# Splitting a 128-point and 16-point transform as 64 points and 32, with the outer steps in half-array TensorE tiles

## The chip, the cores and the metric

The kernel runs on one core of a Trainium2 chip. The metric is device time in microseconds (us) of one execution; lower is better. Three runs of the kernel before were timed, and one more execution was recorded by the hardware profiler. All times of instructions below are from that one profiled execution.

## The reference

The kernel computes a layer and all its gradients. `x` is `A_q` (2048 rows of 512), `xn` its layer norm. Part A is a long convolution: `kv = shift(k) * v`, where `shift` is a four-tap causal filter over the rows with weights `A_shift_k`; then every one of the 512 columns of `kv` is convolved causally with its own kernel of 2048 taps, the rows of `A_ssm_k`, by Fourier transforms of length 4096. Part B is a gated feed-forward of width 1376.

```
k_shift = sum over t of k_pad[:, t:t+S, :] * shift_k[:, 3-t]
kv      = k_shift * v
y       = irfft(rfft(kv padded to 2S) * rfft(ssm_k padded to 2S))[:S] + kv * ssm_D
out     = x + xn * y + ((xn @ w_gate) * (xn @ w_up)) @ w_down
```

The outputs are `out` and the gradients of `sum(out * grad_out)` by `A_q`, `A_k`, `A_v`, `A_shift_k`, `A_ssm_k`, `A_ssm_D`, `B_w_gate`, `B_w_up` and `B_w_down`. The gradients of the convolution need three transforms forward (the taps, `kv`, and `dy = grad_out * xn`) and three back (for `y`, for the gradient of `kv`, for the gradient of the taps).

## The kernel before

**Layout.** A matrix of 2048 rows lies in SBUF as 128 partitions of 16 rows: row `s = 16 p + r` is row `r` of partition `p` (`nat`, L219). A load of two of the 16 rows for all partitions (`x_n[:, 2b:2b+2, :]`) is one DMA of 128 pieces of 2 KB. Such loads and stores are issued one by one by SP: `x_b`, `go_b` (L302, L307), `v_b` (L353), `xb` (L543), `vb` (L918), and the stores of `kb`, `dk`, `o` and `e` (L947, L1088, L1107, L1122). The tile `kh` (and `khC` later) holds 16 rows of `k` and the 3 rows before them, which are fetched from the neighbour partition by two further DMAs (`load_k`, L310; `load_kh`, L1126); `dks` gets the 3 rows behind its own from the next partition in the same way (L950).

**The transforms.** The transform of 2048 padded rows is split in two steps, 128 points over the partitions `p` and 16 over `r`.

- Stage 1 forward, `stage1` (L361): for each signal and each `r`, two matmuls with the table `W1`, one for the real and one for the imaginary part (`c`). Each contracts 128 partitions, gives 128 frequencies and 512 columns, into one PSUM bank of `pf`. ACT (for some of the taps' rows DVE) copies `pf` to `fst`, and after every second `r` a DMA stores it to the DRAM tile `FD`. There are 3 signals of 16 rows, 96 matmuls (and two more, of one row, that add `ssm_D` for signal 0, L372).
- Stage 2, `groups` (L737): in 8 groups `g` of 16 frequencies. `g_fwd` (L577) loads `X` from `FD` and multiplies by the table `EF` in tiles of 64 rows and 32 columns, eight of them next to each other. A tile holds two frequencies of 32 inputs, and half of `EF` is zero, written by the masks in `forward` (L137). ACT copies `ps` to `SP`, DVE multiplies the spectra (`g_mul`, L592), and `g_inv` (L606) goes back with the table `EI` in tiles of 32 rows and 64 columns, whose other half is zeroed by `inverse` (L181). The result goes to the DRAM tile `GD`.
- Stage 1 back. `st1p` (L909) makes two rows of `y` or of the gradient of `kv`: for each row two matmuls of the table `IW` with `g`, accumulated over real and imaginary part, 512 columns, into `pq`; 64 matmuls in all. `inv_dk` (L961) makes the gradient of the taps, transposed: there `g` is the stationary operand and `IW` the moving one, 128 columns, two accumulated matmuls for each piece of `po`; 128 matmuls.
- `kernel_spec` (L408) transposes the taps into that layout first, 64 transposes `ptk` of 128 by 128, in four groups of 16.

**Tables.** The class `Tables` makes `W1`, `IW`, `EF` and `EI` on the chip: phases as integers by DVE (for the inverse by POOL: `inverse_base`, `inverse_phases`), folded to the period by DVE (`fold`, L72), then a sine on ACT (`sin`, L75), then the masks on DVE.

**Order.** The program is written as generators. `main` (L853) walks the eight row chunks of the feed-forward (`ffn1`, `yb`), and after each piece a `side` generator is advanced: first `front` (L712: norm, filter, stage 1 forward), then `groups`. The last part is `dw` (L1014: the weight gradients, `pu` and `pd`), with four side generators that start and step at fixed counts (L1158): `inv_y`, `dsk_gram`, `inv_dk` and `ew`, the elementwise tail `final` and `bwd` on DVE. The first microseconds run under a manual schedule (L657); elsewhere the framework orders each engine's instructions at build time by program order, readiness and priority (`high_priority`). Every engine and SP's DMA queue then work in that fixed order. PSUM is shared by three two-bank buffers (`P2`) and two one-bank buffers (`P1`); `pf`, `ptk`, `ps`, `pg`, `pq`, `po`, `pu`, `pk` and the transposes `pt` all rotate through `P2`.

Of the kernel before, what the change touches and what calls it, by code (L numbers as in the profile page):

```python
# [10 lines left out]
I32 = mybir.dt.int32  # L11
# [22 lines left out]
class Tables:  # L34


    def __init__(self, nc, tab, spectral, tmp):
# [9 lines left out]
        self.odd = tmp.tile([P, P], F32, name="odd")  # L47
        nc.gpsimd.iota(self.odd[:], [[2, P]], base=1, channel_multiplier=0, **f)
        self.lin = tmp.tile([P, P], F32, name="lin")
        nc.gpsimd.iota(self.lin[:], [[1, P]], base=0, channel_multiplier=0, **f)  # L50
        self.patF = tmp.tile([P, 32, 16], F32, name="patF")
        nc.gpsimd.iota(self.patF[:], [[8, 32], [512, 16]], base=0, channel_multiplier=0, **f)
        self.patR = tmp.tile([P, 16, 16], F32, name="patR")
        nc.gpsimd.iota(self.patR[:], [[0, 16], [1, 16]], base=0, channel_multiplier=0, **f)
        self.patG = tmp.tile([P, 16], F32, name="patG")
        nc.gpsimd.iota(self.patG[:], [[32, 8], [4, 2]], base=0, channel_multiplier=0, **f)
# [20 lines left out]

    def small_phases_w(self):
        nc = self.nc
        tmp = self.tmp  # L80
        self.tiw = tmp.tile([P, 2, P], I32, name="tiw")
        for c, off in enumerate((128, 256)):
            nc.vector.tensor_scalar(self.tiw[:, c, :], self.odd[:], self.pf[:, 0:1], float(off + 256), op0=ALU.mult, op1=ALU.add)
        self.fold(self.tiw, 512)

    def small_phases_v(self):
        nc = self.nc
        tmp = self.tmp
        kk = self.col("kk")
        nc.vector.tensor_scalar(kk[:], self.pf[:], 2.0, 1.0, op0=ALU.mult, op1=ALU.add)  # L90
        self.tiv = tmp.tile([P, 2, P], I32, name="tiv")
        for c, off in enumerate((128, 256)):
            nc.vector.tensor_scalar(self.tiv[:, c, :], self.lin[:], kk[:, 0:1], float(off + 256), op0=ALU.mult, op1=ALU.add)
        self.fold(self.tiv, 512)

    def small_sin_w(self):
        self.W1 = self.tab.tile([P, 2, P], BF, name="W1")
        self.sin(self.W1[:], self.tiw, 512)

    def small_sin_v(self):  # L100
        self.IW = self.tab.tile([P, 2, P], BF, name="IW")
        self.iwf = self.tmp.tile([P, 2, P], F32, name="iwf")
        self.sin(self.iwf[:], self.tiv, 512)

    def small_scale(self):
        self.nc.vector.tensor_scalar(self.IW[:], self.iwf[:], 1.0 / 2048, None, op0=ALU.mult)

    def forward_base(self):
# [3 lines left out]
        self.fr = r = self.icol("fr", 0, 15)  # L112
        c = self.icol("fc", 4, 1)
        k4 = self.icol("fk", 5, 3)
        self.fk2 = self.icol("fk2", 5, 1)
        b = self.col("fb")
        nc.vector.tensor_scalar(b[:], k4[:], 2.0, 1.0, op0=ALU.mult, op1=ALU.add)
# [7 lines left out]
    def forward_phases(self):  # L125
        nc = self.nc
        tmp = self.tmp
        self.tif = tmp.tile([P, 32, 2, 16], I32, name="ti", tag="ti")
        for ri in range(2):
            nc.vector.tensor_scalar(self.tif[:, :, ri, :], self.patF[:], self.fr[:, 0:1], self.base[:, ri:ri + 1], op0=ALU.mult, op1=ALU.add)  # L130
        self.fold(self.tif, 8192)

    def forward_sin(self):
        self.zf = self.tmp.tile([P, 32, 2, 16], BF, name="zf")
        self.sin(self.zf[:], self.tif, 8192)

    def forward(self):  # L137
        nc = self.nc
        self.EF = self.spectral.tile([P, 32, 2, 2, 16], BF, name="EF")
        for q in range(2):  # L140
            mk = self.col(f"fm{q}")
            nc.vector.tensor_scalar(mk[:], self.fk2[:], float(q), None, op0=ALU.is_equal)
            nc.vector.tensor_scalar(self.EF[:, :, :, q, :], self.zf[:], mk[:, 0:1], None, op0=ALU.mult)

    def inverse_base(self):

        e = self.nc.gpsimd
        j = self.icol("gj", 0, 15)
        q4 = self.icol("gq", 5, 3)
        self.gk2 = k2 = self.icol("gk", 4, 1)  # L150
        self.gb = b = self.col("gb")
        e.tensor_scalar(b[:], q4[:], 8.0, 1.0, op0=ALU.mult, op1=ALU.add)
        e.tensor_tensor(b[:], b[:], k2[:], op=ALU.add)
        e.tensor_tensor(b[:], b[:], k2[:], op=ALU.add)
        t = self.col("gt")
        e.tensor_scalar(t[:], j[:], 512.0, None, op0=ALU.mult)
        e.tensor_tensor(b[:], b[:], t[:], op=ALU.add)

    def inverse_phases(self):
# [3 lines left out]
        pa = tmp.tile([P, 16, 16], F32, name="pa")  # L163
        e.tensor_tensor(pa[:], self.patR[:], self.patG[:].unsqueeze(2).to_broadcast((P, 16, 16)), op=ALU.mult)
        pb = tmp.tile([P, 16, 16], F32, name="pb")
        e.tensor_scalar(pb[:], self.patR[:], self.gb[:, 0:1], None, op0=ALU.mult)
        e.tensor_tensor(pb[:], pb[:], pa[:], op=ALU.add)
        self.tii = ti = tmp.tile([P, 16, 2, 2, 16], I32, name="tii")
# [8 lines left out]
    def inverse_sin(self):  # L177
        self.zi = self.tmp.tile([P, 16, 2, 2, 16], BF, name="zi")
        self.sin(self.zi[:], self.tii, 8192)

    def inverse(self):  # L181
        nc = self.nc
        self.EI = self.spectral.tile([P, 16, 2, 2, 32], BF, name="EI")
        for q in range(2):
            mk = self.col(f"gm{q}")
            nc.vector.tensor_scalar(mk[:], self.gk2[:], float(q), None, op0=ALU.is_equal)
# [1010 lines left out]
```

## Time and profile before

| What | us |
|---|---|
| the three timed runs | 487.03, 491.52, 493.36 (median 491.52) |
| span of the profiled execution, first to last instruction | 486.7 (its own time is not given beside the span) |
| PE, DVE, ACT, POOL busy | 473.5, 339.5, 318.0, 14.0 |
| L369 `pf`, stage 1 forward: 96 matmuls of 512 columns, PE busy | 25.7 |
| L913 `pq`, stage 1 back: 64 of 512 | 15.1 |
| L971 `po`, stage 1 back for the taps: 128 of 128 | 8.5 |
| L414 `ptk`, transposes of the taps: 64 | 4.7 |
| L584 `ps` and L613 `pg`, stage 2: 384 each of 512, in tiles | 15.0, 15.7 |
| L143 and L187, masks of `EF` and `EI` on DVE | 1.0 each |

The span counts from the first to the last instruction. A matmul's own duration is longer than the distance to the next, because matmuls are pipelined; so what one costs is read from starts. In a list of groups the columns are: line, engine and operation, output and input by the program's names, partitions by elements and type, count; then busy time, mean ns of one, and the idle time of the engine just before them with what ended it. In a timeline the columns are start, length, engine, line, operation, and in brackets an idle time and what ended it. The chain of work that ended last is followed back from the last instruction, at each step to what released it.

### The profile page before, as it was taken

Reading aid. Unit: us, or ns where it says so; the run is one execution under the profiler, and the core shown is the slowest. Engines: PE = TensorE matmul, PEld = TensorE weight load, DVE = VectorE, ACT = ScalarE, POOL = GpSimd, SP = SyncE. Lnnn points to the kernel's source line nnn. Section 1 sums busy time; section 2 is a strip of 40 time slices with the busy share of each in tenths; the row PEclk is TensorE's granted clock in tenths of the full one; section 3 lists DMA queues with packets and bytes.
Section 4 is the critical chain, followed back from the end, with each engine's and each line's share of the span. In section 5 each row is a group of like instructions: output and inputs, shape, how many; then the busy total and the mean of one; then the engine's idle time right before and its main releaser. Section 6 shows DMA issues by size and latency. Waiting matters only on the chain.

```text
span 486.7 us, 10581 instructions
## 1 busy us (share of the span) xinstructions
PE 473.5 (97%) x4375; PEld 316.7 (65%) x4375; DVE 339.5 (70%) x623; ACT 318.0 (65%) x354; POOL 14.0 (3%) x30
## 2 busy tenths in 40 slices
PE   8999998899999999999999999999999999999997
PEld 7867753546747638547547743566767787788885
DVE  6699969987366566777857876113256999999860
ACT  4688885758757769779879976275676544344331
POOL 4400000000000000000000000001000000000000
PEclk9999999999999999999999999999999999999999
DMA  9999999998996968968978469999999999599746
GB/s 273 374 375 336 304 239 308 327 337 323 314 303 218 244 193 275 278 196 261 300 227 270 141 216 351 358 324 318 324 378 377 345 366 410 199 285 252 231 152 193
DMA packets 105325, 139.87 MB, mean 287 GB/s; under 512 B 33307, under 2 KB 78784, under 8 KB 103742
## 3 DMA queue, kind: packets, MB, share of 16 engines
q1 hardware_dynamic: 103694, 137.84, 86.3%
q10 hardware_dynamic: 1584, 1.36, 1.0%
q8 instruction: 34, 0.56, 0.5%
q14 instruction: 13, 0.11, 0.1%
HBM read 68.45 MB, written 63.41 MB: 271 GB/s over the span
## 4 chain that ended last, share of the span: by engine, by line
PE 63%; DVE 21%; DMA 10%; issue 2%; ACT 1%; POOL 1%; SPq 1%; ACTq 0%; DVEq 0%
PE pgu L511 12%; PE px L555 12%; PE pu L1032 10%; PE py L548 6%; PE pdh L517 6%; PE pd L996 5%; DMA x_b<-in_A_q_dram 3%; PE ps L584 3%; PE pg L613 3%; PE pt L840 2%; DMA out_dram<-o 2%; DMA hb<-HDD 2%; DVE t_b L392 2%; DVE ks_b L393 1%; DVE fst L238 1%
## 5 line engine op out<-in xcount | busy, mean ns | idle before, releaser
L555 PE MATMUL px<-WT,hd 128*128 128x512 bf16 (+1 forms) x352 | 81.0, 380 | 0.0
L1032 PEld LDWEIGHTS <-xnC 128*128 128x128 bf16 x704 | 67.1, 98 | 8.8 <-issue 0.9
L555 PEld LDWEIGHTS <-hd 128*128 128x128 bf16 (+1 forms) x352 | 32.9, 98 | 44.2 <-issue 7.3
L1032 PE MATMUL pu<-natd,xnC 128*128 128x256 bf16 x512 | 58.5, 273 | 0.2 <-ACT nath L235 0.2
L235 ACT CAST GO<-pg 128x1024 bf16<-128x1024 f32 x48 | 46.2, 1015 | 13.4 <-issue 6.7
L511 PE MATMUL pgu<-xt,Wu 128*128 128x256 bf16 (+1 forms) x352 | 53.1, 273 | 1.5 <-ACT gu L235 1.0
L600 DVE TENSOR_TENSOR T<-SP 128x2048 bf16<-128x2048 bf16 x24 | 29.4, 1223 | 34.8 <-ACT SP L235 34.8
L235 ACT CAST SP<-ps 128x1024 bf16<-128x1024 f32 x48 | 46.5, 1026 | 10.3 <-PE ps L584 8.4
L235 ACT CAST gu<-pgu 128x1024 bf16<-128x1024 f32 (+1 forms) x48 | 45.3, 944 | 11.6 <-PE pgu L511 11.3
L511 PE MATMUL pgu<-xt,Wg 128*128 128x256 bf16 (+1 forms) x352 | 52.8, 273 | 0.0
L517 PE MATMUL pdh<-gt,WdT 128*128 128x256 bf16 (+1 forms) x352 | 47.4, 273 | 0.1
L511 PEld LDWEIGHTS <-Wu 128*128 128x128 bf16 (+1 forms) x352 | 33.1, 100 | 16.2 <-issue 11.7
L548 PE MATMUL py<-Wd,hd 128*128 128x512 bf16 (+1 forms) x176 | 41.2, 380 | 0.0
L235 ACT CAST fst<-pf 128x1024 bf16<-128x1024 f32 x40 | 38.9, 1028 | 1.5 <-issue 1.3
L235 ACT COPY natd<-pt 128x2048 bf16<-128x2048 bf16 x16 | 30.0, 1874 | 14.1 <-PE pt L840 14.1
L235 ACT CAST og<-pu 128x1024 bf16<-128x1024 f32 (+1 forms) x11 | 10.9, 993 | 42.2 <-PE pu L1032 37.7
L517 PEld LDWEIGHTS <-WdT 128*128 128x128 bf16 (+1 forms) x352 | 34.8, 100 | 5.3 <-ACT WdT L235 0.2
L511 PEld LDWEIGHTS <-Wg 128*128 128x128 bf16 (+1 forms) x352 | 34.9, 100 | 3.6
L532 DVE TENSOR_TENSOR hd<-gu 128x512 bf16<-128x512 bf16 (+1 forms) x48 | 19.0, 396 | 21.8 <-ACT gu L235 21.6
L533 DVE TENSOR_TENSOR hd<-gu,dh 128x1024 bf16<-128x1024 bf16 (+1 forms) x48 | 30.8, 642 | 1.0
L996 PE MATMUL pd<-goC,nath 128*128 128x512 bf16 x128 | 30.1, 379 | 0.0
L548 PEld LDWEIGHTS <-hd 128*128 128x128 bf16 (+1 forms) x176 | 16.5, 98 | 20.8 <-issue 3.1
(173 smaller groups left out, 700.8 us busy)
## 6 DMA issues: line engine op xcount, KB each, us to landing
HDD<-hd SPq DMA_DIRECT2D x35, 384.0 KB, 4.0
FD<-fst SPq DMA_DIRECT2D x24, 512.0 KB, 4.8
X<-FD SPq DMA_DIRECT2D x24, 512.0 KB, 4.3
GD<-GO SPq DMA_DIRECT2D x24, 512.0 KB, 3.6
g<-GD SPq DMA_DIRECT2D x12, 1024.0 KB, 8.6
hb<-HDD SPq DMA_DIRECT2D x8, 1344.0 KB, 8.1
bb<-BX SPq DMA_DIRECT2D x8, 512.0 KB, 6.3
BX<-bx SPq DMA_DIRECT2D x7, 512.0 KB, 4.0
```

Source lines behind the costliest of these rows:

```text
L235: nc.scalar.copy(o, i)
L511: nc.tensor.matmul(pgu[:w, i, t, :], lhsT=W[:, c, f0:f0 + w], rhs=xt[:, :, c, :], start=(c == 0), stop=(c == NC4 - 1))
L517: nc.tensor.matmul(pdh[:w, i, :], lhsT=WdT[:, c, f0:f0 + w], rhs=gt[:, :, c, :], start=(c == 0), stop=(c == NC4 - 1))
L532: nc.vector.tensor_tensor(hd[:fw, fb0:fb0 + n, 0, :], gu[:fw, :n, 0, :], gu[:fw, :n, 1, :], op=ALU.mult)
L533: nc.vector.tensor_tensor(hd[:fw, fb0:fb0 + n, 1:3, :], gu[:fw, :n], dh[:fw, :n].unsqueeze(2).to_broadcast((fw, n, 2, 256)), op=ALU.mult)
L548: nc.tensor.matmul(py[:], lhsT=hd[:fw, fb, 0, ss], rhs=Wd[:fw, fb, :], start=(fb == 0), stop=(fb == NFB - 1))
L555: nc.tensor.matmul(px[:], lhsT=hd[:fw, fb, t, ss], rhs=W[:fw, fb, :], start=(t == 1 and fb == 0), stop=(t == 2 and fb == NFB - 1))
L584: nc.tensor.matmul(ps[32 * q:32 * q + 32, a, :], lhsT=TB.EF[64 * a:64 * a + 64, 4 * g + q, ri].rearrange("p k j -> p (k j)"), rhs=X[64 * a ...
L600: tt(W[:].rearrange("p c a d -> p c (a d)"), A[:, i:i + 1].rearrange("p c a d -> p c (a d)").to_broadcast((P, 2, 2 * D)), B[:].rearrange(" ...
L613: nc.tensor.matmul(pg[q // 2][64 * a:64 * a + 64, q % 2, :], lhsT=TB.EI[32 * q:32 * q + 32, 2 * g + a, yi].rearrange("p k c -> p (k c)"), ...
L996: nc.tensor.matmul(pd[:fw, :], lhsT=nat_h(fb, r), rhs=goC[:, r, :], start=(r == 0), stop=(r == R - 1))
L1032: nc.tensor.matmul(pu[:, c, :, :fw], lhsT=xnC[:, r, cs(c)], rhs=nat_d(fb, r), start=(r == 0), stop=(r == R - 1))
```

## The change

The split becomes 64 points, then 32: row `s = 32 p + 16 h + r` with 64 values of `p`, two of `h` and 16 of `r`, and `h` and `p` together lie on the 128 partitions (`h` selects the half). What follows from it:

- Every load and store of rows becomes two DMAs of 64 partitions (`load_rows`, `store_rows`); the pieces stay 2 KB. The halo of `kh` and `dks` takes three DMAs instead of two. A transposed load of `grad_out` from DRAM becomes two of 64 rows; that of `xn` stays one.
- Stage 1 forward: for each row, two matmuls that contract 64 partitions each, for `h = 0` and `h = 1`, into two banks; one matmul gives the real and imaginary part of 64 frequencies. The count of matmuls and their 512 columns stay.
- Stage 1 back: in `st1p` two matmuls contract 128 partitions each and give 64 outputs, for `h = 0` in the lower and `h = 1` in the upper half of PSUM, with nothing accumulated. In `inv_dk` each matmul has 64 moving columns instead of 128, and writes every second number of `po`.
- The transposes of the taps become 128 of 64 outputs, in the two halves of PSUM.
- `EF` and `EI` are dense: the sine writes them directly, with twice the numbers, and the masks go. Tile shapes and counts of stage 2 stay.
- `inverse_base` and `inverse_phases` are called ahead of the first statistics instead of behind `forward_phases`.

```diff
-        return ap.rearrange("(p r) d -> p r d", r=R)
+        return ap.rearrange("(p h r) d -> h p r d", h=2, r=R)
+    def load_rows(t, src, rb):
+        for h in range(2):
+            nc.sync.dma_start(t[hs(h)], src[h, :, rb, :])
+    def store_rows(dst, rb, t):
+        for h in range(2):
+            last = nc.sync.dma_start(dst[h, :, rb, :], t[hs(h)])
...
-        for c in range(2):
-            point = sig == 0 and r == 0
-            nc.tensor.matmul(pf[:, c, :], lhsT=TB.W1[:, c, :], rhs=src[:, i, :], start=True, stop=not point)
+        for h in range(2):
+            point = sig == 0 and r == 0 and h == 0
+            nc.tensor.matmul(pf[:, h, :], lhsT=TB.W1[hs(h)].rearrange("p k c -> p (k c)"), rhs=src[hs(h), i, :], start=True, stop=not point)
...
-                    src = ssk[:, c, :].rearrange("d (p r) -> d r p", r=R)[:, r0 + i, :]
-                    nc.tensor.transpose(pt[:, i, cs(c)], src, ident[:])
+                    for h in range(2):
+                        src = ssk[:, c, :].rearrange("d (p h r) -> d h r p", h=2, r=R)[:, h, r0 + i, :]
+                        nc.tensor.transpose(pt[hs(h), i, cs(c)], src, ident[:])
...
-            xs, gs = XN[:, rb, :], go_n[:, rb, :]
-        for t, src in ((xt, xs), (gt, gs)):
-            nc.sync.dma_start_transpose(out=t[:].rearrange("p r c s -> p (r c) s"), in_=src.rearrange("p r d -> p (r d)"))
+            xs, gs = XN[:, rb, :], (go_n[0, :, rb, :], go_n[1, :, rb, :])
+        for t, src, ss in ((xt, xs, slice(0, P)), *((gt, g, slice(P // len(gs) * h, P // len(gs) * (h + 1))) for h, g in enumerate(gs))):
+            nc.sync.dma_start_transpose(out=t[:].rearrange("p r c s -> p (r c) s")[:, :, ss], in_=src.rearrange("p r d -> p (r d)"))
...
     TB.forward_base()
+    TB.small_base()
+    TB.inverse_base()
+    TB.inverse_phases()
     norm_stats(0)
...
     TB.forward_phases()
-    TB.inverse_base()
-    TB.inverse_phases()
...
-            TB.forward()
...
-            TB.inverse()
...
-            for c in range(2):
-                nc.tensor.matmul(pq[:, i, :], lhsT=TB.IW[:, c, :], rhs=g[:, c, i0 + i, :], start=(c == 0), stop=(c == 1))
+            for h in range(2):
+                nc.tensor.matmul(pq[hs(h), i, :], lhsT=TB.IW[:], rhs=g[:, h, i0 + i, :], start=True, stop=True)
...
-                DKS[r0] = nc.sync.dma_start(o3_n[:, r0:r0 + 2, :], kb[:])
+                DKS[r0] = store_rows(o3_n, slice(r0, r0 + 2), kb)
...
-                po = P2("po", [P, 2, 4, P])
-                for h in range(2):
+                po = P2("po", [P, 2, 4, 64, 2])
+                for c in range(2):
                     for i in range(4):
-                        for c in range(2):
-                            nc.tensor.matmul(po[:, h, i, :], lhsT=gk[:, c, i, cs(2 * b + h)], rhs=TB.IW[:, c, :],
-                                             start=(c == 0), stop=(c == 1))
+                        for h in range(2):
+                            nc.tensor.matmul(po[:, c, i, :, h], lhsT=gk[:, h, i, cs(2 * b + c)], rhs=TB.IW[:], start=True, stop=True)
```

In the class of the tables, `patF`, `patR` and what is made from them hold 32 numbers where they held 16, `W1`, `IW` and their phases hold half as many as before, and `forward` and `inverse` are gone.

More of the change, by code (lines that the diff above doesn't have):

```diff
@@ L127, in forward_phases @@
         tmp = self.tmp
[L128 removed]
+        self.tif = tmp.tile([P, 32, 2, 32], I32, name="ti", tag="ti")
         for ri in range(2):
@@ L177, in inverse_sin @@
     def inverse_sin(self):
[L178 to L186, printed above, removed]
-            self.last = nc.vector.tensor_scalar(self.EI[:, :, :, q, :], self.zi[:].rearrange("p g y c r -> p g y (c r)"), mk[:, 0:1], None, op0=ALU.mult)
+        self.EI = self.spectral.tile([P, 16, 2, 64], BF, name="EI")
+        self.sin(self.EI[:].rearrange("p g y (c r) -> p g y c r", c=2), self.tii, 8192)
 @with_exitstack
@@ L882 @@
             goC = c1.tile([P, R, D], BF, name="goC")
-            nc.sync.dma_start(goC[:], go_n)
+            load_rows(goC, go_n, slice(0, R))
             nc.sync.dma_start(xnC[:], XN[:])
```

138 lines of the change are left out of this document (69 added, 69 removed).

## The prediction

> **What bounds the kernel now.** I read the page's busy shares first, then the busy time in six stretches (the columns after the stretch: PE, PEld, DVE, ACT, POOL, clock, DMA share, GB/s), and then the chain of work that ended last, to see which engine carries each stretch.
>
> ```profile
> PE 473.5 (97%) x4375; PEld 316.7 (65%) x4375; DVE 339.5 (70%) x623; ACT 318.0 (65%) x354; POOL 14.0 (3%) x30
> ```
>
> ```profile
> 0.00:97.35 97.35, 89.00 (x773) 64.80 (x774) 82.62 (x182) 71.52 (x84) 11.22 (x28) 1.00 0.97 317
> 97.35:125.00 27.65, 27.51 (x164) 16.03 (x165) 20.65 (x39) 20.42 (x26) 0.00 (x0) 1.00 0.94 328
> 125.00:305.00 180.00, 179.53 (x1780) 102.92 (x1778) 121.86 (x169) 139.19 (x170) 0.00 (x0) 1.00 0.81 251
> 305.00:350.00 45.00, 44.89 (x358) 29.37 (x357) 7.50 (x12) 25.51 (x21) 2.74 (x2) 1.00 0.94 337
> 350.00:408.00 58.00, 57.56 (x548) 42.94 (x545) 45.89 (x99) 32.23 (x27) 0.00 (x0) 1.00 1.01 365
> 408.00:487.00 79.00, 74.98 (x759) 60.66 (x759) 61.00 (x125) 29.10 (x29) 0.00 (x0) 1.00 0.76 232
> ```
>
> Up to 97.35 us PE has 8.3 us of idle time and the chain runs almost wholly over DVE and the loads that DVE waits for; from there PE has no gap worth naming. So PE work saved before 97 is worth little, and PE work saved behind it counts, unless something else ends a wait last. One place does so already, at 408 us:
>
> ```profile
> 64.87 7.02 DMA x_b<-in_A_q_dram
> 73.63 3.61 DMA x_b<-in_A_q_dram
> ...
> 97.35 0.60 PE pf L369 x2
> ```
>
> ```profile
> 358.08 0.69 DVE L1106 TENSOR_TENSOR o<-o,bb 128x1024 bf16<-128x1024 bf16 x1 [6.70 <-DMA bb<-BX]
> 371.65 0.69 DVE L1105 TENSOR_TENSOR o<-xnC,yC 128x1024 bf16<-128x1024 bf16 x1 [3.71 <-DMA out_dram<-o]
> ...
> 408.16 0.95 PE L840 MATMUL pt<-ident,hb 128*128 128x128 bf16 x14 [0.60 <-DVE kd L1060]
> ```
>
> From 358.08 DVE works on `final` and `bwd` with two stalls only (0.94 and 3.71 us) until 471, and at 408.16 PE stands still until DVE has read the second `pk` out of PSUM. These two lists (chain, timeline) give the two clocks of the last part: PE's and DVE's.
>
> **What a tiled matmul costs here.** The trace holds both kinds of tile already:
>
> ```profile
> L613 PE MATMUL pg<-T,EI 32*64 32x512 bf16 x384 | 15.7, 387 | 0.5 <-DVE T L603 0.4
> L913 PE MATMUL pq<-g,IW 128*128 128x512 bf16 x64 | 15.1, 379 | 0.0
> L584 PE MATMUL ps<-X,EF 64*32 64x512 bf16 x384 | 15.0, 381 | 0.0
> L971 PE MATMUL po<-IW,g 128*128 128x128 bf16 x128 | 8.5, 219 | 0.0
> L1055 PE MATMUL pk<-khC,dks 128*64 128x256 bf16 x128 | 7.8, 274 | 0.0
> ```
>
> ```profile
> 323.14 1.89 PE L913 MATMUL pq<-g,IW 128*128 128x512 bf16 x8
> 324.87 0.94 PE L840 MATMUL pt<-ident,hb 128*128 128x128 bf16 x14
> ...
> 331.88 3.66 PE L1032 MATMUL pu<-natd,xnC 128*128 128x256 bf16 x32
> 335.37 1.89 PE L996 MATMUL pd<-goC,nath 128*128 128x512 bf16 x8
> ...
> 409.16 1.94 PE L1055 MATMUL pk<-khC,dks 128*64 128x256 bf16 x32
> 411.03 3.67 PE L1032 MATMUL pu<-natd,xnC 128*128 128x256 bf16 x32
> 414.63 1.94 PE L1055 MATMUL pk<-khC,dks 128*64 128x256 bf16 x32
> ```
>
> Read the starts. Full array: 8 matmuls of 512 in 1.73 us, 0.216 each; 32 of 256 in 3.49 us, 0.109 each. The 32 half-column `pk` of 256 take 1.87 us: 16 pairs at 0.109 make 1.74, so two halves run side by side. The 64-row tiles of L584 do too (384 would need 83 us one by one and keep PE busy for 15.0). But going in and out of tiles costs: the `pu` ahead of a `pk` takes 3.60 instead of 3.49, and the `pk` group 0.13 over its pairs, together **0.23 us a group**.
>
> **The change, part by part.** Everything is summed against the profiled span, 486.7 us. The page gives no other time of that execution; the fastest of the three runs is 0.3 above the span, the median 4.8. I put differences on the median, 491.5.
>
> *Stage 1 forward (L369).* 96 matmuls become 48 pairs of 64-row tiles. A group of four costs 4 x 0.216 = 0.87 now, and 2 x 0.216 + 0.23 = 0.66 after: 0.2 saved. A group of two (0.43 to 0.45) saves nothing. Behind 97 us the timeline shows 7 groups of four: -1.4. The groups ahead of 97 lie beside the DVE chain: 0. If pairs didn't overlap, each group would lose 0.23.
>
> *Stage 1 inverse (L913).* Eight groups of 8 cost 1.73; after, 4 x 0.216 + 0.23 = 1.10, 0.63 saved each, 5.1 in all, all before 383 us. What of it reaches 408? PE would stand there 5.1 earlier, DVE not: DVE's run begins with the load of `bb`, issued at 351.80 behind the `g` load, which waits for the fourth `pq` group (4 x 0.63 = 2.5 earlier), and behind two `kb` stores, which become four (+0.33 each, 0.7). DVE is so 1.8 earlier, less 0.2 for halved loads: **-1.6 at 408**; the wait of 0.60 grows to about 4. Bounds: -1.6 to -5.1.
>
> *`po` (L971).* 128 matmuls of 128 columns become 128 of 64; no tiles, the same weight loads. A group of 16 takes 0.89 (448.52 to 449.42 in the timeline), 56 ns each; L1032 at 192 and 256 columns takes 82 and 109 ns, so the time goes with the columns: 29 ns, 0.43 a group, 8 groups behind 408 where PE alone bounds: **-3.4**. Unknown: whether a weight load every 29 ns and an output with a gap of one number hold that pace; the other end is 0. I take the near end: the rows go by columns alone, at one weight load each.
>
> *`ptk` (L414).* 64 transposes become 128 in half-column tiles: a group now takes 1.00 us; after it takes 1.0 + 0.23 if halves overlap, 2.2 if the strided weight loads (149 ns against 98) don't. Four groups between 27 and 49 us, where PE has under 2 us idle: +0.9 to +4.9 of PE work, +1 on the chain.
>
> *Tables.* The inverse phases move ahead of the first statistics. On DVE that puts two small instructions (0.3) into the 1.18 us in which it waits for `x_b`; on POOL only the two memsets stand ahead; no DMA moves. Start on POOL goes from 11.3 to about 6.2 (iotas +0.9 us), the work from 6.2 us to 11 to 12.4 us (L172: 864 ns for 256 numbers, about 190 of it fixed), ready 0 to 1.5 us earlier than 18.67. The fold (0.69) and the sine (1.06), on the chain, double to about 1.2 and 1.93: +1.4. Together 0 to +1.6, I take +0.8. The masks (L142, L143, L186, L187) leave the DVE chain: -2.2. The longer first sine (+0.9) is covered by the 3.99 us in which ACT waits for the second; without that cover it would cost its 0.9.
>
> *Loads and stores in halves.* Some 83 more DMAs on SP, at 0.33 to 0.6 us of issue each. `x_b`, `go_b`, `v_b`, `xb` and the `dk`, `o`, `e`, `kb` stores are named by SP's waits; behind 97 us they have lead and SP is busy for under half of the time (busy issuing about 4 to 8 us in 20), so 0, but about 0.5 at each late load if that lead is gone. Ahead of 97 they stand on the chain three times: the first `x_b` (+0.4), the one at 64.87 with `go_b` ahead of it (+0.9), the one at 73.63 (+0.8): +2.1. The transposed `gt` load becomes two; SP issues one for 2.71 us at 65.86, and halves cost 0 to 2.7 more, with 1.3 us idle behind them: +0.3.
>
> The Trainium skill, "DMA: Bandwidth & Descriptors", section "Rules for kernel authors", speaks against this part: two transfers to disjoint partition halves serialize, so one transfer of 128 partitions is better. By it alone a split load lands a whole fixed cost later, which no run here prices; the sum above charges issue time only.
>
> *Sum:* tables +0.8 - 2.2, `ptk` +1, loads +2.4 make **+2.0** in front; then -1.4, -1.6, -3.4: **-4.4**, 482.3 on the profiled span and 487.1 on the median.
>
> The Trainium skill, "TensorE: Matmul & The Clock Gate", Part 3, prices a packed span as one matmul plus about 4 ns a tile. By it there is no price for entering: 1.6 more for the 7 groups behind 97 (the 1.8 more of `pq` would end in the wait at 408), a sum of -6.0 and 485.5. The trace's 0.23 a group decides mine.
>
> **Rivals.**
> 1. *All of it arrives.* DVE's order is built anew and `kd` comes ahead of part of `final`, or `bb` lands earlier; for it speaks that `kd` already sits inside `final` at 406.63, against it that DVE has no idle time from 372 to 408. Front -1, then -1.4, -5.1, -3.4: -10.9, **480.6**.
> 2. *Slower: SP becomes the bound in front.* SP issues in order and is busy for 11.6 us in 60 to 80 us. Some 29 more loads before 140 us (8 each of `x_b`, `go_b`, `v_b`, 3 `xb`, 2 `kh`) at 0.45 and three transposes at up to 2.7 are 21 us of issue in a stretch where loads end DVE's waits at 64.87, 73.63 and 107.71. If half of that, 10.5, falls on the chain instead of 2.4, the time is **495.2**; it decides from about 7 us on, and all 21 give 505.7. Against it: SP waits for DVE and ACT in most of that time.
> 3. *The pairs don't overlap.* Then nine groups behind 97 and eight `pq` groups lose 0.23 each (3.9), `ptk` costs 4 more than I take, front +6, and only `po` gains: **498**. L584 and L1055 speak against it; full width with half the rows is not in the trace.
>
> **How the numbers follow.** Forecast 0.48, rival 1 0.22, rival 2 0.22, rival 3 0.08. The forecast's own range is 483 to 491 (front -1 to +6 with `po` 0 to -3.4). To hold 8 in 10, rival 1 and the nearer half of rival 2 have to be in: 479 to 499. About 2% is what a measurement of this kernel can tell from no change (its three runs lie 1.3% apart), so the bounds are 481.7 and 501.4. Faster: 0.14 of rival 1 and 0.06 of the forecast by the spread of runs, 0.20. Slower: 0.12 of rival 2 and 0.02 of rival 3, 0.14. Within: 0.66.
>
> **What would show it.** `pq` groups 1.10 from start to next start, `pf` groups of four 0.66, `po` groups 0.46; the masks gone; PE's wait for `kd` near 408 grown to about 4 us; PE still without gaps from about 99 to 400; POOL's last phase by 18.7 us. Wrong would be: pairs at 0.43, `po` still at 0.89, no growth of the `kd` wait (rival 1), or DVE waiting for `x_b`, `go_b` or `v_b` for several us more in front (rival 2).

## The result, and the profile after

The changed kernel takes 535.76 us (median of 4 runs, 533.67 to 538.71), against 491.38 for the kernel before beside it: 1.094 times as long, 95% interval 1.086 to 1.103, slower. The profiled execution took 535.96 us, its span is 534.2. Forecast were 487.1, with a range of 479 to 499.

The first line of the page of the changed kernel, then three of its stretches (columns as above: PE, PEld, DVE, ACT, POOL, clock, DMA share, GB/s):

```profile
PE 480.1 (90%) x4438; PEld 316.4 (59%) x4438; DVE 344.6 (65%) x614; ACT 319.9 (60%) x354; POOL 19.1 (4%) x28
```

```profile
97.35:125.00 27.65, 17.50 (x77) 6.71 (x76) 21.81 (x46) 11.69 (x16) 0.00 (x0) 0.83 0.79 249
125.00:190.00 65.00, 53.29 (x432) 32.47 (x431) 35.67 (x60) 36.39 (x47) 0.00 (x0) 0.92 0.83 260
...
372.00:440.00 68.00, 57.87 (x540) 42.42 (x536) 37.41 (x76) 36.43 (x31) 0.00 (x0) 1.00 0.96 297
```

PE, which had no gap from 97 us on, now stands still for about 10 of 27 us, then 12 of 65, then 10 of 68, and after its gaps the granted clock is 0.83 and 0.92. Set side by side by what PE begins, the two traces part in three steps (a chunk of the feed-forward is taken at its first `pdh` matmul; there are 44 in a chunk):

| PE begins | before | after | later by |
|---|---|---|---|
| second chunk of the feed-forward | 34.4 | 43.0 | 8.6 |
| fourth chunk | 127.7 | 136.2 | 8.5 |
| fifth chunk | 160.4 | 189.5 | 29.1 |
| first `pq` | 323.1 | 356.1 | 33.0 |
| last `pk` group | 414.6 | 462.4 | 47.8 |
| last `pu` | 479.7 | 527.0 | 47.3 |

The row of the fourth chunk hides a part of the second step. In the changed kernel PE did 26 `pdh` matmuls of that chunk in a row, ahead of their `pgu`; the chunk's first `pgu` starts at 146.7 against 125.9, 20.8 later. So the second step begins before 136 us, in the stretch from 97 on in which PE already stands still.

In the timeline of the changed kernel one gap of the second step looks like this (columns: start, length):

```profile
113.93 2.57 SPq L497 DMA_TRANSPOSE gt<-in_grad_out_dram  x2
116.55 1.23 SPq L214 DMA_DIRECT2D xb<-in_A_q_dram  x2
...
120.01 1.29 DVE L554 TENSOR_TENSOR bx<-py,xb 128x512 bf16<-128x512 f32 x2 [1.08 <-DMA xb<-in_A_q_dram]
...
120.76 1.87 PE L559 MATMUL px<-WT,hd 128*128 128x512 bf16 x4 [6.97 <-DVE bx L554]
```

PE waits 6.97 us for DVE, DVE for `xb`, and SP issues `xb` only at 116.55, behind the other DMAs of its queue; the pair of halves takes SP 1.23 us, where the kernel before issued the same `xb` whole, in 0.50 us, at 84.92. In the last part PE waits for the load `hb` (8.8 us), for the load `g` (4.7), and once for the store of `kb` (4.1). All of this points to the loads and stores in halves. Three things could make them dear: SP's time to issue them, the order that the framework builds when it reckons with them (for SP, and for the engines too), or the transfer itself.

### The profile page after: what moved, and what is told of

Its sections match the earlier page's. It is cut to its first block, busy times and chain, and to the rows that moved or that the text cites. A ratio compares the mean times of both kernels' runs of the same rounds, so it can differ in the third digit from the quotient of the medians.

```text
span 534.2 us, 10803 instructions
## 1 busy us (share of the span) xinstructions
PE 480.1 (90%) x4438; PEld 316.4 (59%) x4438; DVE 344.6 (65%) x614; ACT 319.9 (60%) x354; POOL 19.1 (4%) x28
## 4 chain that ended last, share of the span: by engine, by line
PE 56%; DMA 15%; SPq 4%; ACT 2%; DVE 2%; issue 1%; DVEq 0%; ACTq 0%
PE pu L1035 12%; PE pgu L515 10%; PE px L559 10%; PE py L552 5%; PE pd L999 5%; DMA hb<-HDD 4%; PE pdh L521 4%; PE pt L843 3%; DMA g<-GD 3%; DMA khC<-in_A_k_dram 3%; DMA GD<-GO 2%; PE pg L617 2%; PE ps L588 2%; DMA xb<-in_A_q_dram 2%; SPq L497 2%; PE po L975 1%
## 5 line engine op out<-in xcount | busy, mean ns | idle before, releaser
L559 PE MATMUL px<-WT,hd 128*128 128x512 bf16 (+1 forms) x352 | 85.8, 394 | 15.3 <-DVE bx L554 14.7
L234 ACT CAST gu<-pgu 128x1024 bf16<-128x1024 f32 (+1 forms) x48 | 45.3, 945 | 13.4 <-PE pgu L515 12.2
L552 PE MATMUL py<-Wd,hd 128*128 128x512 bf16 (+1 forms) x176 | 43.4, 390 | 3.9 <-DVE bx L554 2.3
L515 PEld LDWEIGHTS <-Wu 128*128 128x128 bf16 (+1 forms) x352 | 32.5, 101 | 16.7 <-issue 13.1
L843 PE MATMUL pt<-ident,hb 128*128 128x128 bf16 x336 | 23.9, 227 | 8.8 <-DMA hb<-HDD 8.8
L234 ACT CAST og<-pu 128x1024 bf16<-128x1024 f32 (+1 forms) x11 | 10.9, 995 | 33.3 <-PE pu L1035 25.7
```

The lines of the kernel that those rows point to most:

```text
L234: nc.scalar.copy(o, i)
L515: nc.tensor.matmul(pgu[:w, i, t, :], lhsT=W[:, c, f0:f0 + w], rhs=xt[:, :, c, :], start=(c == 0), stop=(c == NC4 - 1))
L552: nc.tensor.matmul(py[:], lhsT=hd[:fw, fb, 0, ss], rhs=Wd[:fw, fb, :], start=(fb == 0), stop=(fb == NFB - 1))
L559: nc.tensor.matmul(px[:], lhsT=hd[:fw, fb, t, ss], rhs=W[:fw, fb, :], start=(t == 1 and fb == 0), stop=(t == 2 and fb == NFB - 1))
L843: nc.tensor.transpose(pt[:, r, :fw], hs[:, (r % 2) * 128:(r % 2) * 128 + 128], ident[:fw, :fw])
```

## The experiments

Ratios are against the kernel before, run on the same chip, with 95% intervals.

### Is it the halves? (three runs)

`e1_whole`: the changed kernel with undivided DMAs.

```diff
-        for h in range(2):
-            nc.sync.dma_start(t[hs(h)], src[h, :, rb, :])
+        nc.sync.dma_start(t[:], src[:, rb, :])
```


> The changed kernel with every load, store and transposed load of rows undivided again, one DMA each, in the old deal of rows; the tables and the order of sums of the transforms stay the new ones, so the convolution part of the output mixes the wrong rows; amount and form of all engine work are those of the changed kernel. Theory A (issuing halves on SP makes loads late): SP issue falls back to 0.34 to 0.5 us a load, the waits of `px` for `bx` and of the `pu` region for `hb` and `g` go, and the time comes to 483 to 495. Theory B (the order that was built anew for other matmul costs, or C, the tables, `ptk` and the tile work): it stays at 525 to 540.

Measured 490.33, ratio 0.999 (0.996 to 1.003).

`e2_split`: the kernel before with divided ones.

```diff
-        nc.sync.dma_start(x[:], x_n[:, 2 * b:2 * b + 2, :])
+        load_rows(x, x_n, slice(2 * b, 2 * b + 2))
...
```


> The kernel before with its loads, stores, halos and transposed loads of rows divided into two halves of 64 partitions, and nothing else of the change. Theory A: nearly all of the loss, 525 to 545. Theories B and C: 488 to 500.

Measured 539.78, ratio 1.099 (1.095 to 1.103). The two settle it: all of the loss comes with the halves, none without. Theories B and C, as these expectations name them, are out as causes on their own; but in `e2_split` SP's order is built anew too, and so is DVE's, so "order" stays open as a way in which halves cost.

`e4_gt`: the kernel before with only the transposed loads of `grad_out` in halves.

```diff
-            xs, gs = XN[:, rb, :], go_n[:, rb, :]
+            xs, gs = XN[:, rb, :], (go_n[0:64, rb, :], go_n[64:128, rb, :])
```


> The kernel before with only the five transposed loads of `grad_out` divided into two of 64 rows. If the halves of the transposed loads alone make `xb` late (in the changed kernel each half keeps SP for 1.22 to 2.03 us, and 20.7 us are lost between 136 and 189 us, where such loads stand ahead of `xb`): 500 to 515. If it is the many row halves: 490 to 495. Theories B and C: 490 to 493.

Measured 490.53, ratio 0.998 (0.995 to 1.001): no cost of these can be seen.

### Number, form and place (five runs)

`e3_pool`: the second halves from POOL.

```diff
-        for h in range(2):
-            nc.sync.dma_start(t[hs(h)], src[h, :, rb, :])
+        for h, q in enumerate((nc.sync, nc.gpsimd)):
+            q.dma_start(t[hs(h)], src[h, :, rb, :])
```


> The changed kernel with the second half of every load and store of rows issued from POOL's queue instead of SP's. Theory A by issue time on SP: SP has some 0.6 us less for each of about 130 halves, POOL is idle from 19 us on; time 495 to 515 (the halves of the transposed loads stay on SP). If the halves cost in the transfer and not in the issue, or by theory B or C: 525 to 540. POOL's own price for an issue is in no row so far; if it is above 1 us, the front (three pairs of loads on the chain) loses a few us.

Measured 520.50, ratio 1.062 (1.057 to 1.067): 15 us come back, 29 stay, which lies between the two ranges expected. POOL issues a half in 0.52 us. SP's issue time alone does not explain the loss; how much of the 15 us is issue stays open, since the orders of SP and DVE were built anew here too.

`e5_small`: one small extra DMA behind each whole one. `e6_rows`: halves by rows, all 128 partitions.

```diff
+        nc.sync.dma_start(t[:], src[:, rb, :])
+        nc.sync.dma_start(SCR[n], ident[0:64, 0:16])
```
```diff
+        nc.sync.dma_start(t[:, 0:n, :], src[:, rb.start:m, :])
+        nc.sync.dma_start(t[:, n:2 * n, :], src[:, m:rb.stop, :])
```


> The kernel before with all its DMAs whole, and one small extra DMA on SP (64 partitions of 32 bytes, from the identity to a scratch tile in DRAM, that nobody waits for) behind each of the 74 loads and stores of rows. It adds issues to SP and next to nothing to the DMA engines. If the loss is SP's issue time in order: 505 to 540, the more the nearer the small issue comes to the 0.47 to 0.6 us of a half. If the loss lies in the transfer (a half lands later than a whole, or the DMA engines are worse used): 488 to 497.

> The kernel before with the same 74 loads and stores in two DMAs each, but divided by rows: 128 partitions of one row (1 KB pieces) instead of 64 partitions of two rows. If only the number of issues counts: 515 to 545, as with halves of partitions. If the dear form counts (a half of 64 partitions takes 0.466 us to issue alone, a whole of 128 takes 0.332): an issue of one row should stay at 0.33, the added SP time is less than half of that with halves, and the time 495 to 515.

Measured 505.85, ratio 1.033 (1.026 to 1.039), and 493.81, ratio 1.006 (1.003 to 1.009). So the same loads and stores, with as many DMAs and the same bytes, cost 2.9 us in halves by rows where `e2_split` lost 48 with halves by partitions. Why is not settled by these two runs alone: `e6_rows` also kept nearly the early order of the kernel before in front (the fourth `XN` is normalized at 51.8 us, 48.4 before), and `e5_small` got a late one (78.6). SP's issue of one DMA with no other just ahead takes 0.332 us for 128 partitions, however many bytes, and 0.466 for 64 (0.446 even for 32 bytes each); back to back it is about 0.43 and 0.59. The small DMAs, which move next to nothing, lost 13 us by the first `ps` and 0.6 behind `pq`: with their issue, or the order that came with it, the front loses and the last part does not.

`e7_front` and `e8_late`: halves in the front's loads alone, and in all others alone.

```diff
+        load_rows(x, x_n, slice(2 * b, 2 * b + 2))    # e7_front: x_b, go_b, v_b, kh
+        load_rows(xb, x_n, slice(2 * ch, 2 * ch + 2)) # e8_late: xb, vb, goC, khC, kb, dk, o, e
```


> The kernel before with halves of 64 partitions only in the loads of the front part, `x_b`, `go_b`, `v_b` and `kh` (25 more DMAs). If the front is where it is lost: +8 us by 136 us and most of the 20.7 between 136 and 189, because the front's loads are what stands on SP ahead of `xb` there: 505 to 525. If the late loads and stores carry it: 491 to 500.

> The kernel before with halves only in `xb`, `vb`, `goC`, `khC` and the stores of `kb`, `dk`, `o`, `e` (49 more DMAs). If `xb` itself carries the loss between 136 and 189 and the late part its 11 to 18 us: 510 to 530. If the front carries the first: 500 to 510. If the two parts add up, the losses of this run and of the run with halves in front alone come to 45 to 50 together; a sum far below says that SP has a reserve that both together use up.

Measured 516.97, ratio 1.058 (1.047 to 1.068), and 507.39, ratio 1.036 (1.029 to 1.043). By the medians 25 and 15 us, 40 together, a little under the 45 to 50 of two parts that add up: the second step of the table belongs to the front's loads, not to `xb`, where it showed; the third to the late ones.

### Order against price, in the front (five runs)

In the kernel before SP's order has the fourth `x_b` at 28 us and `xb` of the second chunk at 85; in the changed kernel they are at 75 and 116. So the order was changed by itself.

`e9_xbprio` and `e14_early`: the changed kernel with a better order.

```diff
+        with tc.high_priority(offset=SOON):
+            load_rows(xb, x_n, slice(2 * ch, 2 * ch + 2))
```


> The changed kernel, halves and all, with nothing but a higher priority for the load of `xb`. In the kernels that lose some 20 us between 136 and 189 us (changed kernel, halves everywhere, halves in front), SP's order, which is built before the run, has the transposed loads of a later chunk and then `xb` behind the front's loads, at 112 to 116 us; the kernel before has the transposed loads at 66 to 71 and `xb` at 85. With the priority, `xb` of that chunk stands earlier in the order, the next one behind it too. If the place in SP's order costs the 20 us: 512 to 520. If it is the longer issue itself: 530 to 537.

> The changed kernel with halves, and priorities that put the fourth `x_b` load, the transposed loads of the fourth chunk and the `xb` loads early in SP's order, about where the kernel before has them. If the order carries the front's loss (29 us at 190 us): 508 to 520. If the issue of halves carries it, no order helps: 525 to 537, as with the higher priority of `xb` alone (528).

`e13_order` and `e16_serial`: the kernel before, whole DMAs, with a worse one.

```diff
+                with tc.issue_after(VB["T"].ins):      # xb behind the transposed loads
+                with tc.issue_after(VB["XN"].ins):     # e16 alone: x_b behind the XN store
                     load_x(b + 3)
```


> The kernel before, every DMA whole, with three edges that only fix the order of issue on SP: the load of the fourth `x_b` behind the last store of the taps' `FD`, the transposed loads of the fourth chunk behind the last `v_b` load, and the `xb` of the second chunk behind those. So SP's order in front becomes nearly that of the run with halves in front alone, with not one DMA more. If the order that the halves bring about at build time carries the front's loss of 25 us: 508 to 518. If the longer issue of the halves carries it: 490 to 497.

> As the run of the kernel before with SP's order fixed by edges, and one edge more: each load of `x_b` from the fifth on stands behind the store of the normalized `XN` two rows before it, as in the kernels with halves in front (there SP waits for DVE's normalization, and only then issues the next `x_b`; the kernel before issues the next `x_b` first). All DMAs are whole; SP's order in front is now that of the run with halves in front but for a place or two. If the order carries the front's loss, by this loop of load, normalization, store, load: 505 to 517. If each half's own price carries it (0.13 us more of issue and 0.3 us more to the first packet, twice a load): 490 to 498.

`e17_ahead`: the changed kernel with all three places mended.

```diff
+                    XQ[b + 3] = load_q(b + 3)          # ahead of norm(b + 2) and its XN store
```


> The changed kernel with halves, and SP's order put back from three sides: every `x_b` load from the fourth on ahead of the `XN` store that it stood behind, the transposed loads of the fourth chunk early, `xb` with a higher priority. If the loop through the `XN` store carries the front's loss of 29 us: 505 to 518. If the halves' own price does: 524 to 535.

| run | us | ratio |
|---|---|---|
| `e9_xbprio` | 528.39 | 1.076 (1.070 to 1.082) |
| `e14_early` | 529.22 | 1.080 (1.072 to 1.089) |
| `e17_ahead` | 522.02 | 1.063 (1.056 to 1.070) |
| `e13_order` | 493.47 | 1.005 (1.001 to 1.009) |
| `e16_serial` | 493.55 | 1.006 (1.003 to 1.009) |

Between `e8_late` and these runs I had come to hold the order for the cause, because the runs that lost 13 us and more in the front all had the late order. That theory fell: with whole loads the bad order costs 3.6 us, and with halves the mended order wins back 14 of 44. So SP's order alone is not the price. The forecasts of the runs with halves hit less well: `e14_early` is in the range for "no order helps", `e9_xbprio` and `e17_ahead` lie between their two ranges; and in `e17_ahead` the fourth `x_b` loads came only some 1.3 us ahead of the `XN` store (85.6 against 86.9), so the place was hardly mended there. Two kernels with almost the same order on SP can be set side by side. With halves (`e7_front`), one round of the front:

```profile
85.48 0.34 SPq L358 DMA_DIRECT2D XN<-x_b  x1
...
86.35 1.12 SPq L224 DMA_DIRECT2D x_b<-in_A_q_dram  x2
87.51 1.24 SPq L224 DMA_DIRECT2D go_b<-in_grad_out_dram  x2
...
98.08 0.34 SPq L358 DMA_DIRECT2D XN<-x_b  x1
```

and with whole loads (`e16_serial`):

```profile
82.49 0.35 SPq L349 DMA_DIRECT2D XN<-x_b  x1
82.89 0.43 SPq L302 DMA_DIRECT2D x_b<-in_A_q_dram  x1
83.37 0.44 SPq L307 DMA_DIRECT2D go_b<-in_grad_out_dram  x1
...
90.38 0.34 SPq L349 DMA_DIRECT2D XN<-x_b  x1
```

SP loads `x_b`, waits until DVE has normalized it, stores `XN` and only then loads the next. From the fourth `x_b` to the eighth that loop takes 12.9 us a round with halves (71.8 to 123.2) and 9.1 with whole loads (73.3 to 109.7): four rounds make 15. The fourth `x_b` is not late with halves, it is 1.5 us early; the eighth is 13.5 late, its `XN` store 16.7, the first `ps` 18.2, and the sixth chunk 20.7. So most of the difference arises in these rounds.

What a round is longer by is argued, not shown. Three pairs of issues on SP, each about 0.75 us longer, are 2.2 of the 3.8 if they all end waits. But DVE's waits in those rounds (until 137 us with halves, the first two lines; until 120 with whole loads, the last) are not mainly for `x_b`:

```profile
DVE dy_b L391 <- PE pf L378: 4.8, 2, 3.4
DVE ks_b L399 <- DMA KS<-ks_b: 4.8, 2, 3.4
...
DVE stats L334 <- DMA x_b<-in_A_q_dram: 0.7, 1, 0.7
```

```profile
DVE stats L325 <- DMA x_b<-in_A_q_dram: 5.0, 2, 3.2
```

(The columns are the total wait in us, how often, the longest.) DVE waits with halves for PE's `pf` and for the stores `KS` that SP issues. In the four rounds it is busy for 38.1 of 51.4 us with halves and for 33.3 of 36.4 with whole loads: of the 15 us, 4.7 are more DVE work (it had done 8 us less before the fourth `x_b`) and 10.3 are DVE standing still. DVE's order was built anew with the halves, and no run has halves and whole loads under the same order of DVE. That DVE's new order, more than the halves' own price, makes the rounds longer is a rival that no run here settles.

### The last part (four runs)

`e11_prio_pool`: `e9_xbprio` with the stores from POOL. `e15_khpool`: `e8_late` with `khC` from POOL.

```diff
-            last = nc.sync.dma_start(dst[h, :, rb, :], t[hs(h)])
+            last = nc.gpsimd.dma_start(dst[h, :, rb, :], t[hs(h)])
```
```diff
+                nc.gpsimd.dma_start(khC[h, 3:3 + R, :], k_n[h])
```


> As the run with the higher priority of `xb`, and all stores of `kb`, `dk`, `o` and `e` issued from POOL's queue (64 halves, some 36 us of issue) instead of SP's. If the last part's loss (about 18 us from 320 to the end in the changed kernel; 15 with halves in the late loads and stores alone) is SP's issue time ahead of `hb`, `g`, `bb` and `khC`: 8 to 15 us less than that run. If it is the landing of halved loads or the buffers that wait for the stores to land: 0 to 4 us less.

> The run with halves only in the late loads and stores, with the two large halves of `khC` issued from POOL instead of SP. In the built programs each DMA of SP waits for the one eight places ahead of it to have landed (eight semaphores in turn); in that run the stores of `kb` wait 8.6 us for the `khC` halves, which take 12 us to land, and `bb`, `hb` and `g` are queued behind. If this wait for places carries the late loss: 8.6 us less, 497 to 502. If it is the issue time of the many halves: 504 to 508.

Measured 539.09, ratio 1.098 (1.091 to 1.105), and 510.43, ratio 1.042 (1.034 to 1.049). Both miss. `e15_khpool` has the orders of SP and DVE of `e8_late`, so the place eight ahead is not the cause. `e11_prio_pool` decides nothing on SP's issue of the stores, since DVE's order in the last part was built anew there: its trace has PE waiting 17.3 us once for DVE's `kd`, and why it loses 11 more stays open.

`e18_big` and `e19_small8`: halves only in `goC` and `khC`, and only in the six small ones.

```diff
-            nc.sync.dma_start(goC[:], go_n)
+            load_rows(goC, go_n, slice(0, R))
```
```diff
-        nc.sync.dma_start(vb[:], v_n[:, r0:r0 + 2, :])
+        load_rows(vb, v_n, slice(r0, r0 + 2))
```


> The kernel before with halves only in the two loads of 2 MB, `goC` and `khC`: two DMAs more, so no issue time and no places to speak of. In the traces so far a 16 KB piece of such a load takes 651 ns where the load is whole and about 1200 ns where it is halved; over 16 DMA engines that is some 4.5 us more of each engine's time a load, in a stretch (350 to 408 us) in which the DMA engines are busy without a gap. If the time of the pieces carries the last part's loss: 4 to 10 us more than before, 495 to 501. If issue time or places carry it: 490 to 493.

> The kernel before with halves only in `xb`, `vb` and the stores of `kb`, `dk`, `o`, `e` (48 DMAs more). With the small extra DMAs, as many in the last part, nothing was lost there, and with as many halves by rows 4 us. If the time of the pieces carries the loss (a 2 KB piece takes 115 ns instead of 92 in 360 to 410 us; 6144 pieces over 16 engines, about 9 us of each engine): 498 to 503, and the losses of this run and of the run with the two large loads add up to the 15 of both. If the issue of the 48 halves carries all of it: 505 to 508, and the other run nothing.

Measured 497.33, ratio 1.019 (1.013 to 1.024), and 498.55, ratio 1.020 (1.016 to 1.024). Together the two lose 1.9 + 2.0%, the run of both 3.6%; each alone lies at the edge of the 2% at which a change is told from none here. The cleanest comparison is `e8_late` with `e19_small8`: they differ by the halves of `goC` and `khC` alone, and DVE, ACT and POOL have the same order in both, SP the same but for the place of one `xb`. By the ratios that is 8 us for two DMAs more (17.9 against 9.7 lost behind `pq` in the traces). Neither order nor issue time can be that; it is the transfer. For the small halves no run holds the order: DVE's order in the last part was built anew in `e19_small8`. Against the order as their cause stands that `e3_pool`, with nearly the order of the kernel before there, loses 14.0 us behind `pq`, and `e1_whole`, with a new order and whole loads, none.

The page's line of the main DMA queue shows what the transfers take: packets, MB, and the time of the packets as a share of 16 engines' span. Here it is for the kernel before and for `e18_big` (whose profiled execution is its fastest, 492.38):

```profile
q1 hardware_dynamic: 103694, 137.84, 86.3%
```

```profile
q1 hardware_dynamic: 103726, 137.84, 87.4%
```

Times the spans, 486.7 and 490.5, that is 420.0 us of each DMA engine before and 428.7 here, for the same bytes. By the same line it is 436.2 in `e19_small8`, 445.8 in `e8_late` and 451.9 in the changed kernel, but 421.0 with the small DMAs and 426.3 with halves by rows. The losses behind `pq` rise with it, but not strictly: 0.6, 3.8, 1.0, 9.7, 17.9 and 14.4 us in the traces of `e5_small`, `e6_rows`, `e18_big`, `e19_small8`, `e8_late` and the changed kernel. In the packet records a 16 KB piece takes 651 ns between 350 and 410 us where `khC` is whole and 1224 where it is halved (`e8_late`); the 2 KB pieces there average 92 and 119 ns. The prediction's own table has that stretch with a DMA share of 1.01: by this count the DMA engines had nothing to spare.

The Trainium skill, "SBUF — State Buffer", section "Door 1: The DMA port swizzle", says that a transfer over partitions 0 to 63 reaches 8 of 16 ports, and gives 196 GB/s against 328 for 128 partitions at 1 MiB. An estimate from these two figures is that a piece takes 1.7 times as long; the 16 KB piece takes 1.9 times as long, the 2 KB pieces, of which many are of other transfers, 1.3 times. The Trainium skill, "DMA: Bandwidth & Descriptors", section "Rules for kernel authors", says that two transfers to disjoint partition halves serialize, from two queues too. `e3_pool`, still 6.2% slower with the second halves from POOL, would fit that, but no run here shows two halves going one after the other.

### What the change would give with whole loads

`e12_whole_ptk`: `e1_whole` with the old `ptk`.

```diff
-                    for h in range(2):
-                        nc.tensor.transpose(pt[hs(h), i, cs(c)], src, ident[:])
+                    nc.tensor.transpose(pt[:, i, cs(c)], src, ident[:])
```


> As the run with whole loads in the old deal of rows, with the 64 transposes `ptk` of the kernel before instead of the 128 halves; again the convolution part of the output mixes the wrong rows. That run is 2.6 us later than the kernel before when the first `pq` starts, where the prediction's steps without loads gave 1.8 earlier (tables -1.4, `ptk` +1, stage 1 forward -1.4). If the halved transposes make the difference (1.97 us a group against 1.00): 1.5 to 4 us less than that run, 486 to 489, and the first `ps` 2 to 4 us earlier. If it is the order of the front's loads or the tables: no change, 489 to 491.

Measured 488.23, ratio 0.994 (0.991 to 0.997). Against `e1_whole` that is 2.8 us less by the ratios, 2.1 by the medians, 1.0 by the two profiled executions, and the intervals of the two ratios touch: the halved transposes cost some 1 to 3 us. PE's part of it is 4 groups by 0.93 us, 3.7. But the first `ps` stays 2.6 us later than before, so the front's lateness is not theirs. Where that 2.6 comes from stays open. As this change needs its loads and stores in halves, none of these runs shows a version of it that beats the kernel before.

## Why the prediction was wrong, step by step

**The step that failed: "behind 97 us they have lead and SP is busy for under half of the time ..., so 0", and "+2.1" in front.** Halves cost 48 us (`e2_split`), priced at 2.4: 25 in the front's loads, 15 in the others, each alone.
- In front, the prediction had the halves on the chain three times, for their issue alone (+2.1). `e7_front` lost 25 us. Its trace, against `e16_serial`, has each of four rounds of load, normalization, `XN` store and next load 3.8 us longer; why a round is that much longer is shown in part only. The second rival had 10.5 or 21 us in front; `e7_front` less what its order costs with whole loads (25 - 3.6, `e16_serial`) is 21.4. Its place was right, its mechanism not: SP is not the bound there, it waits for DVE for 16.4 us between 70 and 137. None of the rivals came near the whole: the dearest price named, 505.7, is 30 us short.
- Behind 97 us, "busy issuing about 4 to 8 us in 20" does not hold in the prediction's own trace: SP issues for 11.4 us in 100 to 120, 12.8 in 120 to 140, 10.9 in 380 to 400, and 12.2 and 14.0 in the two stretches from 420 to 460. And SP's idle time was not all that counted: the DMA share of 1.01 in the prediction's own table spoke against the 0 behind 320, and no step used it. `e8_late` with `e19_small8` shows 8 us there for the transfer of two large loads.
- The rule of the Trainium skill on halves ("DMA: Bandwidth & Descriptors", section "Rules for kernel authors") was weighed and left out of the sum.
- The same 4438 matmuls keep PE busy for 480.1 us in the changed kernel and 468.8 in `e1_whole`. So of the 46.8 us between the two spans, 35.5 are more idle time of PE, and 11.3 are matmuls that took longer; where that shows, the granted clock was lower (0.50 from 120.76 to 125.70, behind a gap).

**The other steps can be read in `e1_whole`, without the halves.** Its page and timeline:

```profile
34.64 1.99 PE L414 MATMUL ptk<-ident,ssk 128*64 128x128 bf16 x32
36.57 0.64 PE L511 MATMUL pgu<-xt,Wu 128*96 128x256 bf16 x4
...
47.33 0.60 PE L368 MATMUL pf<-kn,W 64*128 64x512 bf16 x4
47.87 0.61 PE L511 MATMUL pgu<-xt,Wu 128*128 128x256 bf16 x4
...
322.13 3.62 PE L994 MATMUL pd<-goC,nath 128*128 128x512 bf16 x16
325.68 1.05 PE L912 MATMUL pq<-g,IW 128*64 128x512 bf16 x8
326.67 0.95 PE L839 MATMUL pt<-ident,hb 128*128 128x128 bf16 x14
```

- *`pf` and `pq`: right.* Start to next start they take 0.54 and 0.99 us, and the group ahead of each takes some 0.09 longer than its matmuls alone (the 16 `pd` 3.55 us, where 16 by 0.216 are 3.46): 0.63 and 1.08, predicted 0.66 and 1.10. Pairs overlap; the third rival is out for these. (The stretch behind 97 has six groups of four `pf` in the timeline before, not seven; that moves the sum by 0.2.)
- *Tables: right.* In `e1_whole` POOL's last phase ends at 17.7 us (18.7 before), the masks are gone, the longer sine takes 1.91, and ACT goes on 0.3 us later than before, predicted +0.8.
- *What reaches 408: right in size, by luck.* From first to last `pq` 4.2 us are saved, behind the first `pk` groups 1.5 are left, predicted 1.6. What takes the rest is some 4 us, as predicted, but not a wait for `kd`:

```profile
350.00:408.00 58.00, 54.00 (x531) 40.06 (x528) 43.83 (x94) 31.65 (x26) 0.00 (x0) 1.00 0.97 350
```

PE stands still for 4.0 us there, 1.7 of them for `khC`, 1.0 for `g`, and the rest is the beginning of a wait of 1.6 for `hb`: loads were next in line.
- *`ptk`: dearer than taken.* A group takes 1.93 us (1.23 predicted with overlap, 2.2 without), 1.00 before. That is 3.7 us of PE work in the bounds of 0.9 to 4.9, of which 1 was taken; `e12_whole_ptk` saves some 1 to 3.
- *`po`: wrong.* The near end (-3.4) was taken, the far end (0) came. In the changed kernel a group of 16 still takes 0.86 us:

```profile
495.88 1.06 PE L975 MATMUL po<-IW,g 128*128 128x64 bf16 x16
496.74 1.49 PE L999 MATMUL pd<-goC,natT 128*128 128x512 bf16 x6
```

54 ns each, against 56 before, with one weight load of 128 columns a matmul, whether 64 or 128 columns move. The prediction's rule that the time goes with the columns, read at 192 and 256, does not hold down here. That the weight load sets it fits these lines, but no run took it apart.

In sum these steps without the halves made -6.8 (the sum of -4.4 without the loads' 2.4). `e1_whole` is even with the kernel before, its profiled span 0.7 longer. Of the 7.5 between, `po` is 3.4, and 4.3 are there already at the first `pq`, which comes 2.5 later where the steps made 1.8 earlier. That lateness stays with the old `ptk` too, so its cause is open.

## What to carry to other kernels

Before dividing a load over partitions, price it by a run that divides that load alone: here halves by partitions cost 48 us and halves by rows 2.9. Look at the DMA share of the stretches where the load runs, since a half took the DMA engines more time for the same bytes, and where the share was near 1 two such loads cost 8 us. Look also for a queue that is closed to a loop by a store that waits: there a round that gets longer counts each time, and the queue's idle time is not all reserve. Read how long the queue is busy in each stretch, not on average. A group of small matmuls with a weight load each gained nothing here from going from 128 moving columns to 64.

And when two kernels are compared, compare the order of every engine: a change of a DMA rebuilt DVE's order as well, and the comparison that kept all orders is the one that settled something.

## What the runs showed of the hardware that was not expected

- A DMA of 64 partitions takes SP longer to issue than one of 128 (0.466 against 0.332 us), and its first packet starts later: a store's 1.12 us after the issue begins against 0.83, by the packet records.
- Divided by rows instead of partitions, the same loads and stores cost 2.9 us in place of 48 (`e6_rows`, `e2_split`; their orders differ too).
- A 16 KB piece of `khC` took 651 ns whole and 1224 ns halved, and the DMA engines' time for the same 137.84 MB rose from 420.0 to 451.9 us each in the changed kernel.
- Halved transposes with the identity hardly overlap: a group of 32 with 64 outputs took 1.93 us, one of 16 with 128 outputs 1.00.
- In the gap of 6.97 us of PE in the changed kernel (to 120.76 us) and behind it the granted clock was 0.50 from about 115.5 to 125.7 us, some 5 us past the gap's end, and 0.99 after that; over 97 to 125 us this makes the 0.83. The 22 `px` matmuls there take 7.3 us, 4.85 before.
